# Spreading a row by one fp32 matmul, new shares in the first K'V, and later loads of a fourth batch

## The chip, the cores and the metric

The kernel runs on one core of one Trainium2 chip. A core has a matmul engine (TensorE, PE in the profile; its weight loads are PEld), three engines for elementwise work (VectorE or DVE, ScalarE or ACT, GpSimd or POOL), a queue engine (SyncE or SP) and 16 DMA engines that all queues share. The engines run side by side, each through its own list of instructions in order, and wait for each other through semaphores. The metric is the device time of one execution in microseconds (us); less is better. Before the change three runs took 333.25, 333.89 and 334.29 us.

## What is computed

Linear attention with cosine-weighted features, followed by a gated feed-forward layer:

```python
# attention: B, H, S, D = 8, 8, 576, 64
def phi(x, c, s):
    r = np.maximum(x, 0.0)
    return np.concatenate([r * c, r * s], axis=-1)
q_p = phi(q, cos_w, sin_w); k_p = phi(k, cos_w, sin_w)
kv  = np.einsum('bhsf,bhsd->bhfd', k_p, v)
z   = np.sum(k_p, axis=2)
num = np.einsum('bhsf,bhfd->bhsd', q_p, kv)
den = np.einsum('bhsf,bhf->bhs', q_p, z)[..., None] + 1e-06
x   = (num / den)              # as 4608 tokens x 512
# feed-forward: 512 -> 1536 -> 512
rms = np.sqrt(np.mean(x * x, axis=-1, keepdims=True) + 1e-06)
xn  = x / rms * rms_g
g, val = xn @ w_gate, xn @ w_val
out = (g * sigmoid(g) * val) @ w_out
```

## The kernel before

The 4608 tokens are handled as nine blocks of 512 tokens, each of four tiles of 128; block 8 collects the fifth half tiles of the batches. A block is 12 steps (`step`, L693): each makes one 128x512 piece of the gate product (`gps`) and of the value product (`vps`), applies silu on ScalarE (L714) and multiplies on VectorE (L724). From block 2 on each step also issues four matmuls of the output product of the block before (L520). Blocks 0 to 4 cut their steps into parts of 128 or 256 token columns (`PARTS`, L682), so that a block can start before all its tiles are there: block 1 (steps 12 to 23) works in steps 12 to 17 on tiles 0 and 1 and from step 18 on needs tiles 2 and 3 too.

Attention work of later batches is hung into these steps by a plan written by hand (`at`, L535): in step g, slot "pe" stands behind the step's matmuls, "dve0", "act1" and so on stand at places between. A tile goes through `num_mm` (product of turned q features and K'V, L379), `divide` (L417), `sumsq` (ScalarE squares, L428, then a power on GpSimd, L433), `norm` (L438, which multiplies by the gains `gb`) and a transpose of the normed tile, either on TensorE (`x_turn_pe`, L456, with an eviction) or as a DMA transpose on SP's queue (`x_turn`, L446). Turned q features come the same two ways (`q_turn_pe`, L355 and evictions L364 and L366; `q_turn`, a DMA transpose on SP, L344).

Loads of k, q and v (`load`, L112, each two DMAs) go to SP's queue for batch 0 and from batch 4 on, to GpSimd's queue for batches 1 and 2, and for batch 3 k and v go to GpSimd and q to SP. GpSimd's list holds nothing but constants, the weight loads, these loads and the powers of `sumsq`, in program order. k, q and v have two buffers each, used by even and odd batches. Between blocks 0 and 1 `lead` (L737) prepares batch 1, issues most of block 0's output matmuls, and issues the loads of batch 3's k and v.

The opening, ahead of step 0, prepares batch 0. VectorE builds the angle table, ScalarE takes its sine (L193), then both make k features (L271 and L269) and q features. Loads, features and K'V of batch 0 are cut in two halves of four heads (`HALVES`). TensorE runs 44 warming matmuls on constants meanwhile. The row of gains `rms_g` (1x512) has to stand on all 128 partitions: GpSimd splits it into three bf16 parts (L224, L226), three matmuls by a column of ones add them up on all partitions (L231), and ScalarE copies the sum into `gb` (L234). Then two q tiles are turned on TensorE; v is cast to bf16 (`v_cast`, tiles 0 to 2 on VectorE, L283, tiles 3 and 4 on ScalarE, L281); `kv_half` (L325) multiplies the five token tiles of four heads in the order 0, 1, 3, 2, 4 and evicts the half on VectorE (L337). ScalarE's copy of the second turned q tile (L366) stands between its casts of the two halves. Instructions recorded with `K` keep their program order on each engine.

Of the kernel before, what the change touches and what calls it, by code (L numbers as in the profile page):

```python
# [10 lines left out]
FP32 = mybir.dt.float32  # L11
BF16 = mybir.dt.bfloat16
AF = mybir.ActivationFunctionType
ALU = mybir.AluOpType
# [3 lines left out]
def kernel(  # L18
# [11 lines left out]
    nc = tc.nc  # L30
    B, H, S, D = q.shape
    DM = H * D
    DFF = moe_w_gate.shape[1]
    P = 128
# [12 lines left out]
    def K(i):  # L47
        tc.keep_in_program_order(i)
        return i

    consts = ctx.enter_context(tc.tile_pool(name="consts", bufs=1))
# [25 lines left out]
    def gv_tile(shape, dtype, name):  # L77
        u = gv_out.pop(0)
        t = ps_gv.tile(shape, dtype, name=name, tag=f"gv{u}")
        gv_in[id(t)] = (u, t)  # L80
        return t

    def gv_read(t):

        if id(t) in gv_in:
            gv_out.append(gv_in.pop(id(t))[0])
# [25 lines left out]
    def load(t, src, b, odd_five=False, cuts=(0, NC5), hs=slice(0, H), eng=None):  # L112
        if eng is None:
            eng = nc.gpsimd if 0 < b < 3 or b == 3 and src is not q else nc.sync
        for lo, hi in zip(cuts[:-1], cuts[1:]):
            for par, t0, jn in lanes(odd_five):
                z = min(hi, jn)
                if z <= lo:
                    continue
                K(eng.dma_start(  # L120
                    out=t[par:P:2, hs, lo * D : z * D],
                    in_=src[b, hs, :, :].rearrange("h (i j) d -> i h (j d)", j=NT)[
                        :, :, (t0 + lo) * D : (t0 + z) * D
                    ],
                ))

    def load_v(b, cuts=(0, NC5)):
        load(vraw[b], v, b, False, cuts)

    def load_k(b):  # L130
        load(kraw[b], k, b)
# [6 lines left out]
    clear_fifth(vbuf[0], nc.vector)  # L138
    gb = consts.tile([P, DM], FP32, name="gb")

    NX = 3
    xbuf = [consts.tile([P, DM + 1], FP32, name=f"x{u}") for u in range(NX)]
    g1, grest = xbuf[1][0:1, 0:DM], xbuf[2][0:1, 0:DM]
    K(nc.scalar.dma_start(out=g1, in_=moe_rms_g.rearrange("(o d) -> o d", o=1)))
    for hs in HALVES:
        load(kraw[0], k, 0, hs=hs)
# [1 line left out]
    for hs in HALVES:  # L148
# [14 lines left out]
        out=odd_i[:, :], in_=iota_i[:, :], scalar=1, op=ALU.bitwise_and  # L163
# [10 lines left out]
        out=iota_f[:, :], in0=iota_f[:, :], scalar1=J + 0.5, scalar2=None, op0=ALU.mult  # L174
    )
    for u, half in ((0, 0.5), (1, -0.5)):
        nc.vector.scalar_tensor_tensor(
            out=first[:, u : u + 1], in0=odd_f[:, :], scalar=half, in1=iota_f[:, :],
# [3 lines left out]
            out=th[:, 1, u * J : (u + 1) * J], in0=row_f[:, :],  # L182
# [3 lines left out]
        out=th[:, 1, 2 * J : NT], in0=first[:, 1:2],  # L186
# [3 lines left out]
        out=th[:, 0, :], in_=th[:, 1, :], scalar=math.pi / 2.0, op=ALU.add  # L190
# [14 lines left out]
    NK = 6  # L205
# [4 lines left out]
    kvm = [consts.tile([P, H, E], BF16, name=f"kvm{u}") for u in range(NK)]  # L210

    for u in range(NX):
        nc.gpsimd.memset(xbuf[u][:, DM : DM + 1], math.sqrt(1e-6 * DM))
    warm = consts.tile([P, 2 * P], BF16, name="warm")

    nc.vector.memset(warm[:, :], 1.0)
    for j in range(NC5):
        nc.gpsimd.memset(vx[j][:, :, D:E], 1.0)


    gpart = [kvm[NK - 1 - u][0:1, :, :].rearrange("p h e -> p (h e)")[:, 0:DM] for u in range(3)]
    for u in range(3):
        rest = g1 if u == 0 else grest
        K(nc.gpsimd.tensor_copy(out=gpart[u], in_=rest))  # L224
        if u < 2:
            K(nc.gpsimd.tensor_tensor(out=grest, in0=rest, in1=gpart[u], op=ALU.subtract))  # L226

    def spread_gains():
        ps = gv_tile([P, DM], FP32, "gains")
        for u in range(3):  # L230
            K(nc.tensor.matmul(  # L231
                ps[:, :], lhsT=warm[0:1, 0:P], rhs=gpart[u], start=(u == 0), stop=(u == 2)
            ))
        K(nc.scalar.copy(out=gb[:, :], in_=ps[:, :]))  # L234
        gv_read(ps)

# [38 lines left out]
    def k_feat(b, j, c, act=False, hs=slice(0, H)):  # L275
        feat(kp[j][:, hs, c, :], kraw[b][:, hs, j * D : (j + 1) * D], table(c, 0, j), act)

    def v_cast(b, j, act=False, hs=slice(0, H)):
        src, dst = vraw[b][:, hs, j * D : (j + 1) * D], vx[j][:, hs, 0:D]
        if act:  # L280
            K(nc.scalar.copy(out=dst, in_=src))  # L281
        else:
            K(nc.vector.tensor_copy(out=dst, in_=src))  # L283
# [18 lines left out]
    def kv_head(bank, j, h, start, stop):  # L302
        K(nc.tensor.matmul(  # L303
            bank[:, (h % Z) * E : (h % Z) * E + D + 1],
            lhsT=kp[j][:, h, :, :].rearrange("p c d -> p (c d)"),
            rhs=vx[j][:, h, 0 : D + 1],
            start=start, stop=stop,
        ))
# [16 lines left out]
    def kv_half(z, dve):  # L325

        bank = gv_tile([P, TB], FP32, "kv0")
        order = (0, 1, 3, 2, 4)
        for j in order:
            for h in range(z * Z, (z + 1) * Z):  # L330
                kv_head(
                    bank, j, h, j == order[0] and h % Z == 0, j == order[-1] and h % Z == Z - 1
                )
        src = bank[:, 0 : Z * E].rearrange("p (s w) -> p s w", w=E)[:, :, 0 : D + 1]
        dst = kvm[0][:, z * Z : (z + 1) * Z, 0 : D + 1]
        if dve:
            K(nc.vector.tensor_copy(out=dst, in_=src))  # L337
        else:
            K(nc.scalar.copy(out=dst, in_=src))
        gv_read(bank)  # L340
# [10 lines left out]
    def q_turn_pe(b, t):  # L351
        ps = gv_tile([P, H, P], BF16, "qtp")
        qp = qps.pop((b, t))
        for h in range(H):
            K(nc.tensor.transpose(  # L355
                ps[:, h, :], qp[:, h, :, :].rearrange("p c d -> p (c d)"), ident_b[:, :]
            ))
        qtp[b, t] = ps

    def q_evict(b, t, dve=False):  # L360
        tt = rqtp.tile([P, H, P], BF16, name="rqT", tag="rqT")
        ps = qtp.pop((b, t))
        if dve:
            K(nc.vector.tensor_copy(out=tt[:, :, :], in_=ps[:, :, :]))  # L364
        else:
            K(nc.scalar.copy(out=tt[:, :, :], in_=ps[:, :, :]))  # L366
        gv_read(ps)
        rqT[b, t] = tt
# [41 lines left out]
    def divide(key):  # L410
# [3 lines left out]
        r = recs.pop(key)[:, :].rearrange("p (z s) -> p z s", z=2)  # L414
        x = xbuf[nx[0] % NX]
        nx[0] += 1
# [118 lines left out]
    def at(g, w, f, *a):  # L535
        plan[g, w].append(lambda: f(*a))
# [100 lines left out]
        tile_at(22 + t, (2, t), 2, t)  # L637


    at(16, "pe", load_q, 3)  # L640
    for j in range(NC5):
        for c in range(2):
            at(22 + j, "act2" if c else "dve1", k_feat, 3, j, c, c == 1)
# [93 lines left out]
    def lead():  # L737

        for j in range(NC5):
            for c in range(2):  # L740
                k_feat(1, j, c, act=(j > 2))
        outs(0, 18)
        for t in range(2):
            for c in range(2):
                q_feat(1, t, c, act=(c == 1))
        q_turn_pe(1, 0)
        q_evict(1, 0, dve=True)
        outs(18, 21)
        q_turn_pe(1, 1)
        for j in range(NC5):  # L750
            v_cast(1, j, act=(j == 1))
        q_evict(1, 1)
        outs(21, 24)
        for j in range(NC5):
            kv_mm(1, j, j == 0, j == NC5 - 1)
        kv_evict(1)
        q_feat(1, 2, 0)
        q_feat(1, 2, 1, act=True)
        outs(24, 27)
        num_mm((1, 0))  # L760
        num_mm((1, 1))
        q_feat(1, 3, 1, act=True)
        divide((1, 0))
        sumsq((1, 0))
        outs(27, 31)
        q_turn_pe(1, 2)
        divide((1, 1))
        sumsq((1, 1))
        outs(31, 36)
        q_evict(1, 2, dve=True)  # L770
        q_feat(1, 3, 0)
        norm((1, 0))
        outs(36, 40)
        q_turn_pe(1, 3)
        load_k(3)
        load_v(3)
        x_turn_pe((1, 0))
        x_evict((1, 0), 1, 0, dve=True)
        q_evict(1, 3)
        outs(40, 45)  # L780
        norm((1, 1))
        x_turn_pe((1, 1))
        x_evict((1, 1), 1, 1, dve=True)
        for j in range(2):
            k_feat(2, j, 1, act=True)
        outs(45, 48)
        num_mm((1, 2))
# [4 lines left out]
    def warm_up(n):  # L792
        for _ in range(n):
            K(nc.tensor.matmul(
                wps[:, 0 : 2 * P], lhsT=warm[:, 0:P], rhs=warm[:, :], start=True, stop=True
            ))

    warm_up(44)
    for hs in HALVES:
        for j in range(NC5):  # L800
            for c in range(2):
# [7 lines left out]
    load_q(0, (J, NC5), eng=nc.gpsimd)  # L809
    for c in range(2):  # L810
        load_wo(c)
    spread_gains()
    q_turn_pe(0, 0)
    q_evict(0, 0, dve=True)
    q_turn_pe(0, 1)
    for z, hs in enumerate(HALVES):
        for j in range(NC5):
            v_cast(0, j, act=(j > 2), hs=hs)
        if z == 0:
            q_evict(0, 1)  # L820
        kv_half(z, True)
    num_mm((0, 0))
    num_mm((0, 1))
    for c in range(2):
# [27 lines left out]
    for c in range(2):  # L852
# [5 lines left out]
        for nn in range(NNT):  # L858
            K(nc.tensor.matmul(
                last[:, cs], lhsT=hT[B][:, nn, (J - 1) * P : J * P], rhs=wo[:, nn, cs],  # L860
                start=(nn == 0), stop=(nn == NNT - 1),
# [36 lines left out]
```

## Time and profile before

| what | value |
|---|---|
| three runs, median | 333.89 us (333.25 to 334.29) |
| the profiled execution | 332.95 us, of which the span is 331.1 us |
| first gate matmul of step 0 | 21.20 us after the span's start |
| TensorE between 9.84 us and 21.20 us | waits in six places |
| step 12 (block 1) starts | 59.48 us |
| step 18 starts | 71.07 us |
| DMA queue of SP (q1) | 72800 packets, 40.12 MB |
| DMA queue of GpSimd (q0) | 7168 packets, 14.29 MB |

How to read it: the span is what the profiler saw from the first instruction to the last; the run's time includes what lies around it. In the rows that follow, a line of the timeline gives start, duration, engine, source line, operation, tiles out and in, count, and in brackets the idle time ahead of it with what ended that. A line of the chain of waits gives start, length and the work that held up the end at that time. A row of DMA issues gives the tiles, the queue, the kind, how many, and the median time in us from issue to landing. A row of stretches gives the stretch, its length, busy time (with the count of instructions that touch it), granted TensorE clock, busy share of the DMA engines and GB/s.

### The profile page before, as it was taken

The numbers are of one execution on the slowest core, as the hardware profiler recorded it, in microseconds if no ns is written. First come the engines' busy times: TensorE is split into PE (matmuls) and PEld (weight loads), VectorE is DVE, ScalarE is ACT, GpSimd is POOL, SyncE is SP. The second block draws the span as 40 slices with busy tenths as digits, with TensorE's granted clock in tenths as the row PEclk, the third lists the DMA queues.
The fourth block names the chain that finished last, engine by engine and source line by source line (L and its number), as shares of the span: only waits on it lengthen the run. The fifth ranks groups of instructions, "written<-read, shape, count | busy, mean of one in ns | idle before, by whom it ended". The sixth has DMA issues, their size and how long they took to land.

```text
span 331.1 us, 7177 instructions
## 1 busy us (share of the span) xinstructions
PE 317.1 (96%) x2802; PEld 210.5 (64%) x2837; DVE 194.1 (59%) x403; ACT 168.8 (51%) x324; POOL 47.4 (14%) x90
## 2 busy tenths in 40 slices
PE   6679999999999999999999999999999999999995
PEld 4469966999887777778777644454444444444443
DVE  8786367777966585677867676746543422223200
ACT  3853477857864366575646564644432322322221
POOL 8664343200101000001110001000100000000000
PEclk9999999999999999999999999999999999999999
DMA  7999999994258999995799898254224020000012
GB/s 207 266 206 215 285 335 384 359 228 88 44 124 257 276 288 325 182 333 100 172 242 277 170 234 134 76 85 111 50 71 105 34 61 33 34 32 32 34 63 96
DMA packets 80164, 55.00 MB, mean 166 GB/s; under 512 B 51265, under 2 KB 73553, under 8 KB 80130
## 3 DMA queue, kind: packets, MB, share of 16 engines
q1 hardware_dynamic: 72800, 40.12, 50.1%
q0 software_dynamic: 7168, 14.29, 17.0%
q8 instruction: 22, 0.36, 0.5%
q10 hardware_dynamic: 162, 0.13, 0.1%
q14 instruction: 12, 0.10, 0.1%
HBM read 37.75 MB, written 9.44 MB: 142 GB/s over the span
## 4 chain that ended last, share of the span: by engine, by line
PE 86%; DVE 7%; issue 2%; DMA 2%; ACT 1%; POOL 0%; ACTq 0%; DVEq 0%
PE acc L520 26%; PE gps L488 14%; PE vps L488 14%; PE gps L475 12%; PE vps L475 12%; PE att L379 3%; PE att L303 3%; DMA xnT<-xn 2%; DVE kp L271 2%; DVE xn L438 1%; PE qtp L355 1%; PE xps L456 1%; DVE x L417 1%; DMA out_dram<-osb 1%; DVE vx L283 1%
## 5 line engine op out<-in xcount | busy, mean ns | idle before, releaser
L724 DVE TENSOR_TENSOR hT<-vps,sil 128x512 bf16<-128x512 f32 x108 | 74.5, 690 | 97.8 <-PE vps L475 58.0
L714 ACT ACTIVATE sil<-gps 128x512 bf16<-128x512 f32 x108 | 64.4, 596 | 98.6 <-PE gps L475 59.8
L520 PE MATMUL acc<-wo,hT 128*128 128x512 bf16 x396 | 101.8, 379 | 1.4 <-ACT osb L526 0.2
L520 PEld LDWEIGHTS <-hT 128*128 128x128 bf16 x420 | 40.5, 98 | 40.2 <-issue 0.3
L488 PE MATMUL gps<-xnT,wg 128*128 128x256 bf16 (+1 forms) x608 | 62.5, 250 | 1.2 <-DVE xnT L463 0.5
L488 PE MATMUL vps<-xnT,wv 128*128 128x256 bf16 (+1 forms) x608 | 62.5, 250 | 0.0
L488 PEld LDWEIGHTS <-wg 128*128 128x128 bf16 x608 | 48.0, 98 | 8.6 <-issue 1.2
L488 PEld LDWEIGHTS <-wv 128*128 128x128 bf16 x608 | 49.4, 98 | 4.1
L433 POOL TENSOR_TENSOR rs<-ss,mhalf 128x1 f32<-128x1 f32 x36 | 20.4, 567 | 197.0 <-ACT sq L428 197.0
L475 PE MATMUL gps<-xnT,wg 128*128 128x512 bf16 x139 | 36.7, 379 | 0.4
L475 PE MATMUL vps<-xnT,wv 128*128 128x512 bf16 x141 | 36.5, 379 | 0.1
L526 ACT COPY osb<-acc 128x512 f32<-128x512 f32 x35 | 20.5, 585 | 31.5 <-PE acc L520 28.7
L475 PEld LDWEIGHTS <-wv 128*128 128x128 bf16 x192 | 18.8, 98 | 22.7
L438 DVE SCALAR_TENSOR_TENSOR xn<-x,rs,gb 128x512 bf16<-128x512 f32 x36 | 26.9, 748 | 7.3 <-POOL rs L433 7.3
L475 PEld LDWEIGHTS <-wg 128*128 128x128 bf16 x192 | 18.0, 98 | 20.1
L428 ACT ACTIVATE sq<-x 128x513 f32<-128x513 f32 x36 | 22.6, 628 | 10.6 <-DVE x L417 8.6
L417 DVE TENSOR_TENSOR x<-att,rec 128x512 f32<-128x512 f32 x36 | 24.9, 691 | 1.3
L271 DVE TENSOR_SCALAR kp<-kbuf,trig 128x512 bf16<-128x512 f32 (+1 forms) x56 | 23.5, 457 | 0.6 <-PE att L303 0.3
L271 DVE TENSOR_SCALAR qp<-qbuf,trig 128x512 bf16<-128x512 f32 x50 | 22.8, 478 | 0.0
L269 ACT ACTIVATE kp<-kbuf,trig 128x512 bf16<-128x512 f32 (+1 forms) x34 | 21.4, 663 | 0.0
L269 ACT ACTIVATE qp<-qbuf,trig 128x512 bf16<-128x512 f32 x30 | 21.0, 712 | 0.4 <-DMA qbuf<-in_q_dram 0.4
L379 PEld LDWEIGHTS <-rqT 128*128 128x128 bf16 x320 | 14.3, 98 | 8.5 <-DVE rqT L364 1.4
(68 smaller groups left out, 195.1 us busy)
## 6 DMA issues: line engine op xcount, KB each, us to landing
out_dram<-osb SPq DMA_DIRECT2D x70, 128.0 KB, 2.1
qbuf<-in_q_dram SPq DMA_DIRECT2D x5, 640.0 KB, 6.2
qbuf<-in_q_dram SPq DMA_DIRECT2D x5, 512.0 KB, 5.0
kbuf<-in_k_dram SPq DMA_DIRECT2D x4, 640.0 KB, 6.4
vbuf<-in_v_dram SPq DMA_DIRECT2D x4, 640.0 KB, 6.9
kbuf<-in_k_dram SPq DMA_DIRECT2D x4, 512.0 KB, 5.3
vbuf<-in_v_dram SPq DMA_DIRECT2D x4, 512.0 KB, 6.1
kbuf<-in_k_dram POOLq DMA_DIRECT2D x3, 640.0 KB, 10.3
```

Source lines behind the costliest of these rows:

```text
L269: K(nc.scalar.activation(out=dst, in_=src, func=AF.Relu, scale=scale))
L271: K(nc.vector.tensor_scalar(out=dst, in0=src, scalar1=scale, scalar2=0.0, op0=ALU.mult, op1=ALU.max,))
L379: K(nc.tensor.matmul(nums[key][:, h // Z, (h % Z) * E : (h % Z) * E + D + 1], lhsT=rqT[a, t][:, h, :], rhs=kvm[a % NK][:, h, 0 : D + 1], s ...
L417: K(nc.vector.tensor_tensor(out=x[:, 0:DM].rearrange("p (z s d) -> p z s d", z=2, d=D), in0=a[:, :, :, 0:D], in1=r.unsqueeze(3).to_broadca ...
L428: K(nc.scalar.activation(out=sq[:, :], in_=xs[key][:, :], func=AF.Square, scale=1.0 / math.sqrt(DM), accum_out=ss[:, :],))
L438: K(nc.vector.scalar_tensor_tensor(out=xn[:, :], in0=xs.pop(key)[:, 0:DM], scalar=rss.pop(key)[:, :], in1=gb[:, :], op0=ALU.mult, op1=ALU. ...
L475: K(nc.tensor.matmul(ps[:, :], lhsT=w[:, dt, nn * P : (nn + 1) * P], rhs=xnT[blk][:, dt, :], start=(dt == 0), stop=(dt == NDT - 1),))
L488: K(nc.tensor.matmul(ps[:, i * cn : (i + 1) * cn], lhsT=w[:, dt, (n0 + i) * P : (n0 + i + 1) * P], rhs=xnT[blk][:, dt, c0 : c0 + cn], star ...
L520: K(nc.tensor.matmul(acc[blk][:, :], lhsT=hT[blk][:, nn, jt * P : (jt + 1) * P], rhs=wo[:, nn, :], start=(nn == 0), stop=(nn == NNT - 1),))
L526: K(nc.scalar.copy(out=osb[:, :], in_=acc[blk][:, :]))
L714: K(nc.scalar.activation(out=sil[:, :], in_=gp[:, :], func=AF.Silu))
L724: K(nc.vector.tensor_tensor(out=dst, in0=a, in1=c, op=ALU.mult))
```

## The change

The gains are spread by one fp32 matmul of a 1x128 row of ones by the 1x512 row itself; the five GpSimd operations that split the row are gone. It stands behind 14 warming matmuls, and 32 more follow, where 44 stood ahead of the three matmuls. So ScalarE's copy into `gb` now precedes its k features in the list. Of v's first half ScalarE casts three tiles and VectorE two; of the second half it stays two and three. The first half of K'V is evicted by ScalarE, the second by VectorE. The order of the token tiles is 0, 2, 1, 3, 4 in the first half and 0, 3, 1, 4, 2 in the second. Four warming matmuls stand ahead of K'V and four between its halves. ScalarE's copy of the second turned q tile comes behind both halves. The loads of batch 3: k and v move from `lead` to the ends of steps 16 and 17, q from step 16 to step 19. In GpSimd's list k's and v's four loads thus stand behind two more powers (tiles (1,2) and (1,3)); in SP's list q's two loads stand behind one more DMA transpose of q features.

```diff
-    g1, grest = xbuf[1][0:1, 0:DM], xbuf[2][0:1, 0:DM]
+    g1 = xbuf[1][0:1, 0:DM]
...
-    gpart = [kvm[NK - 1 - u][0:1, :, :].rearrange("p h e -> p (h e)")[:, 0:DM] for u in range(3)]
-    for u in range(3):
-        rest = g1 if u == 0 else grest
-        K(nc.gpsimd.tensor_copy(out=gpart[u], in_=rest))
-        if u < 2:
-            K(nc.gpsimd.tensor_tensor(out=grest, in0=rest, in1=gpart[u], op=ALU.subtract))
+    ones = consts.tile([1, P], FP32, name="ones")
+    nc.vector.memset(ones[:, :], 1.0)
 
     def spread_gains():
         ps = gv_tile([P, DM], FP32, "gains")
-        for u in range(3):
-            K(nc.tensor.matmul(
-                ps[:, :], lhsT=warm[0:1, 0:P], rhs=gpart[u], start=(u == 0), stop=(u == 2)
-            ))
+        K(nc.tensor.matmul(ps[:, :], lhsT=ones[:, :], rhs=g1, start=True, stop=True))
         K(nc.scalar.copy(out=gb[:, :], in_=ps[:, :]))
         gv_read(ps)
...
     def kv_half(z, dve):
-        order = (0, 1, 3, 2, 4)
+        order = (0, 3, 1, 4, 2) if z else (0, 2, 1, 3, 4)
...
-    at(16, "pe", load_q, 3)
+    at(16, "pe", load_k, 3)
+    at(17, "pe", load_v, 3)
+    at(19, "pe", load_q, 3)
...
         q_turn_pe(1, 3)
-        load_k(3)
-        load_v(3)
         x_turn_pe((1, 0))
...
-    warm_up(44)
+    warm_up(14)
+    spread_gains()
+    warm_up(32)
     for hs in HALVES:
         for j in range(NC5):
             for c in range(2):
...
     for c in range(2):
         load_wo(c)
-    spread_gains()
     q_turn_pe(0, 0)
     q_evict(0, 0, dve=True)
     q_turn_pe(0, 1)
+    warm_up(4)
     for z, hs in enumerate(HALVES):
         for j in range(NC5):
-            v_cast(0, j, act=(j > 2), hs=hs)
+            v_cast(0, j, act=(j > 2 - (z == 0)), hs=hs)
+        kv_half(z, z == 1)
         if z == 0:
-            q_evict(0, 1)
-        kv_half(z, True)
+            warm_up(4)
+    q_evict(0, 1)
     num_mm((0, 0))
```

## The prediction

> **What bounds the kernel now.** I read the page first (busy shares), then the chain of waits with its times, then the stretches where TensorE is not the bound: the opening (0 to 21 us) and one gap near 71 us.
>
> ```profile
> span 331.1 us, 7177 instructions
> PE 317.1 (96%) x2802; PEld 210.5 (64%) x2837; DVE 194.1 (59%) x403; ACT 168.8 (51%) x324; POOL 47.4 (14%) x90
> ```
>
> TensorE is busy 96% of the span, so only 14 us are open to any change that leaves its main work alone. The chain of waits says where they lie:
>
> ```profile
> 11.15 0.62 PE qtp L355 x8
> ...
> 12.40 0.81 DVE vx L283 x2
> ...
> 14.31 1.13 DVE vx L283 x3
> ...
> 15.48 0.43 PE kv L303 x8
> ...
> 15.93 0.44 DVE kvm L337
> ...
> 65.55 5.39 DMA xnT<-xn
> ```
>
> Until 21.20, where the first expert matmul starts, the chain runs on VectorE: key features, the copy of the turned q tile, six casts of v, two evictions of K'V, then divide and norm. After that it is TensorE, but for one DMA transpose, of tile (1,3), issued at 65.55 and landing at 70.94. The timeline shows what TensorE lost there, and what was issued around it:
>
> ```profile
> 60.04 1.11 SPq L510 DMA_DIRECT2D out_dram<-osb  x2
> 63.95 2.78 SPq L446 DMA_TRANSPOSE xnT<-xn  x2
> ...
> 64.18 0.55 POOL L433 TENSOR_TENSOR rs<-ss,mhalf 128x1 f32<-128x1 f32 x1 [1.76 <-ACT sq L428]
> ...
> 71.07 1.03 PE L488 MATMUL gps<-xnT,wg 128*128 128x256 bf16 x8 [0.45 <-DMA xnT<-xn]
> ```
>
> TensorE waited 0.45 us at step 18, so it would have started at 70.62. The ScalarE timeline of the opening:
>
> ```profile
> 10.23 1.32 ACT L269 ACTIVATE qp<-qbuf,trig 128x512 bf16<-128x512 f32 x2
> 11.46 0.56 ACT L234 COPY gb<-gains 128x512 f32<-128x512 f32 x1
> 11.92 0.71 ACT L281 CAST vx<-vbuf 128x256 bf16<-128x256 f32 x2
> 12.54 1.00 ACT L366 COPY rqT<-qtp 128x1024 bf16<-128x1024 bf16 x1
> ```
>
> Start to start, a q feature costs 0.62 us here, the copy of the gains 0.46, a cast 0.31, the q copy 0.90.
>
> **The change, part by part.** *Splitting of the row.* Five GpSimd operations between 2.08 and 7.83 go. GpSimd's next deed with a follower is the probe at 11.07, which waits for VectorE's q feature, so this is worth nothing; if the probe waited for GpSimd, it would be worth up to 4 us of GpSimd's time. The memset of ones sits in VectorE's angle chain, which ends in the sine at 6.77: between 0.10 us (a 128x1 memset) and 0.27 (the 128x256 one); I take 0.1.
>
> *The fp32 matmul.* No fp32 matmul stands in this trace. The warming matmuls price the clock of that moment by their starts (the granted clock reads 1.00 throughout):
>
> ```profile
> 3.50:4.50 1.00, 1.00 (x7) 1.00 1.03 358
> ...
> 8.50:9.50 1.00, 1.00 (x12) 1.00 1.06 375
> ```
>
> All 44 take 7.03 us, early ones some 0.21 us apart, late ones 0.11, so 14 end near 5.75. Below, fp32 costs one 512-column pass at the early rate, 0.42. Above, both operands in three bf16 parts make nine products, 3.8. The nearest row is the three passes that it replaces (0.82 us late, twice that early); I take 1.3 for a place where the rate changes: done at 7.1. The copy of the gains now stands ahead of all key features on ScalarE, behind the sine (6.77 plus 0.1 and 0.22), so those start at 7.2 + 0.46 = 7.66 and not 7.02: 0.64 later. ScalarE had the time idle, 4.22 us ahead of the sine, but the order puts the copy behind it.
>
> [...]
>
> *Casts and evictions.* ScalarE's first q feature now ends at 10.89 + 0.64 = 11.53, so the turn of q tile 0 starts at 11.58 instead of 11.15, and VectorE, which copies it first, begins its casts at 12.83 instead of 12.40. It has two, then three, and no eviction between: at 0.36 each the first half's end at 13.60, the second's at 14.68 (15.44 before). ScalarE's second q feature ends at 12.15, its three casts near 13.1. TensorE then has 12 of 20 matmuls left (0.69 us for 16, so some 0.5 with their latency): K'V of the first half at 14.15, its eviction on ScalarE until 14.6 (0.43, by VectorE's row), then ScalarE's two casts until 15.26. The last eight matmuls take 0.43: eviction of the second half at 15.73 and not 15.93. That is -0.2 us on the chain. Behind ScalarE's wait for K'V stand its two casts, which TensorE then waits for, and the q copy (ends 16.2, just when its product is due). Bounds: with ScalarE out of the way VectorE's casts alone set it, 12.40 + 5 x 0.36 = 14.2 against 15.44, -1.2; with the 3.8 us matmul ScalarE is 2.5 us later still, +2.
>
> *Warming matmuls.* Two more ahead, four and four between: eight at 0.11 fall into TensorE's waits (1.33 us for the vx casts at 12.75 and 14.74). Cost 0; without that cover, 0.45 us each four.
>
> *Loads of batch 3.* Four K and V loads on GpSimd's queue (56.45 to 59.22) are moved behind the two powers of tiles (1,2) and (1,3). GpSimd waits for no step, only for its own order: they issue from the end of that power, 64.73, until 67.5, not in steps 16 and 17 proper. Each takes 0.69 us to issue. q's two loads move behind one rqT transpose on SP that starts at 76.39: landing near 78 + 6.6, while its first reader is at 86.60; K and V have first readers at 81.11. Both fit, so nothing is late there. What matters is step 18. The second transpose issues at 65.55, 0.8 us behind the first K load, as both hang on the same power. Landing times, issue to landing, of the same transpose:
>
> ```profile
> xnT<-xn SPq DMA_TRANSPOSE x3, 7.0
> ...
> xnT<-xn SPq DMA_TRANSPOSE x5, 2.4
> ```
>
> The first is from 110 to 130 us, among loads; the second from 200 to 240, quiet. The two stores at 60.04 took 7.4 us beside these same K and V loads, against 2.1 as the page's median: 5.3 more. Quiet, it lands at 67.95 and the 0.45 us go: the bound below. With 5.3 more on 2.4 it lands at 73.25. I take 7.3, the longest of the three transposes: 72.85, a wait of 2.23 at step 18, 1.78 more than now. The gap widens, since 2.3 MB at the 355 GB/s seen take 6.6 us from about 66.5. The rqT transpose behind it (landing 4.9 now) is needed at 75.99, later still by then.
>
> Sum: -0.2 + 1.78 = +1.6 us. The profiled execution took 332.95 (span 331.1 and 1.85 around it); it would take 334.5. The median of the runs shown, 333.89, is 0.94 above it, so I forecast 335.5.
>
> **The rivals.** *Quick transposes* (not slower): the second transpose is through before K's packets come, or takes turns with them without loss. [...] Against: the stores at 60.04. It gives -0.2 - 0.45 = -0.65, 333.2. [...]
>
> *Quick transposes and a free ScalarE* (faster): if the fp32 pass is over before the sine and ScalarE's operations end sooner, the opening gains up to 1.2: -1.2 - 0.45 = -1.65, 332.2.
>
> *A long fp32 matmul* (slower, in another place): from 2.6 us on, the copy of the gains holds ScalarE's key features past 8.9, and TensorE's turn of q past 12.8. At 3.8 us: +2 - 0.45 = +1.55, 335.4.
>
> *The loads stay where they were*, because GpSimd runs ahead: excluded, since two powers stand before them.
>
> **How the numbers follow.** Transpose caught behind K and V (forecast) 0.50, 335.5, its own range 334.3 to 337.2; quick transposes 0.18, 333.2; with free ScalarE 0.20, 332.2; long matmul 0.12, 335.4. The range reaches from 332.4 to 337.2: below lies a part of the third case, above the two slow cases together. A change within 0.3% (1.0 us) can't be told from none. Faster by more: the third case and a little of the second, 0.22; slower by more: the first and fourth but for their low ends, 0.60; between, 0.18.
>
> **What would show it.** Right: the two xnT transposes of 63.95 and 65.55 land over 6 us after issue, and the first gps matmul of step 18 waits 2 us or more for DMA. Wrong: that wait is gone. The opening is read at the first gps matmul (21.20), the copy of gb (behind the sine, at 7.2), the second K'V eviction (15.73). A second wait at the product of tile (2,0) would add to it. If the total rises with these as before, a load of batch 3 came late for its first reader.

## The result and the profile after

The changed kernel takes 344.15 us (median of 6 runs, 343.62 to 345.91) where the kernel before took 334.03 (333.25 to 334.94) beside it: a ratio of 1.0316, interval 1.0284 to 1.0349. Forecast were 335.5 us and at most 337.2. Comparisons leave out disturbed executions; one of these is the profiled execution of the run after_kv_sp below, which is why no view of that run is read.

The profiled execution took 345.82 us. Its page, busy time by engine and the granted clock in 40 slices of 8.6 us:

```profile
span 344.1 us, 7192 instructions
...
PE 322.7 (94%) x2811; PEld 213.5 (62%) x2846; DVE 190.7 (55%) x402; ACT 169.5 (49%) x326; POOL 43.4 (13%) x85
...
PE   6979999935999999999999999999999999999995
...
PEclk9999999995999999999999999999999999999999
```

The span is 13.0 us longer, TensorE's busy time only 5.6. In the ninth and tenth slice (69 to 86 us) TensorE stands idle and then runs at a lower clock. The chain of waits (start, length, what held up the end) has that stretch as one DMA transpose, and the opening above it:

```profile
2.81 3.17 PE wps L786 x14
5.98 2.00 PE gains L225 x2
7.98 5.28 PE wps L786 x32
13.26 0.46 PE qtp L347 x8
...
22.44 1.05 PE gps L480 x16
...
66.79 14.70 DMA xnT<-xn
81.49 0.14 issue
81.63 1.87 PE gps L480 x8
83.49 1.71 PE vps L480 x8
85.20 1.87 PE att L295 x40
87.06 0.87 PE gps L480 x8
```

The transpose of tile (1,3) was issued at 66.79 and landed 14.70 us later, where it took 5.39 before. Behind it eight gate matmuls take 1.87 us, eight value matmuls 1.71, and 40 of K'V 1.87; in the chain of the kernel before the same three are 1.03, 0.87 and 1.27. The timeline names the partners (times, engine, line, tiles; in brackets the idle time ahead):

```profile
65.20 2.78 SPq L438 DMA_TRANSPOSE xnT<-xn  x2
...
65.93 1.50 POOL L120 DMA_DIRECT2D kbuf<-in_k_dram  x2
...
67.43 1.37 POOL L120 DMA_DIRECT2D vbuf<-in_v_dram  x2
...
81.63 1.87 PE L480 MATMUL gps<-xnT,wg 128*128 128x256 bf16 x8 [9.77 <-DMA xnT<-xn]
```

The first transpose landed in 2.5 us, ahead of the loads' packets. The second met them. The view of DMA issues (queue, kind, count, KB, us from issue to landing) shows that both sides lost:

```profile
kbuf<-in_k_dram POOLq DMA_DIRECT2D x1, 640.0 KB, 9.2
vbuf<-in_v_dram POOLq DMA_DIRECT2D x1, 640.0 KB, 13.5
...
rqT<-qp SPq DMA_TRANSPOSE x1, 14.1
```

V's second load, issued near 68.1, landed near 81.6, just as the transpose did (81.49). The DMA engines had work meanwhile. The stretches (length, busy time of each engine, clock, DMA share, GB/s), first after, then before:

```profile
60.00:72.00 12.00, 11.86 (x211) 11.41 (x209) 10.15 (x22) 8.04 (x16) 3.92 (x6) 1.00 0.56 126
72.00:81.00 9.00, 0.00 (x0) 0.00 (x0) 1.66 (x4) 0.82 (x2) 0.00 (x0) 0.74 1.01 175
81.00:90.00 9.00, 8.37 (x91) 7.11 (x92) 2.10 (x6) 3.45 (x7) 0.00 (x0) 0.70 0.10 14
```

```profile
60.00:72.00 12.00, 11.55 (x203) 11.31 (x201) 10.47 (x22) 7.95 (x16) 1.11 (x2) 1.00 1.15 277
```

From 72 to 81 us they show a full share of busy time, yet move 175 GB/s; before, at a like share, 277. So packets took longer, rather than waiting for work. The loads' packets can be priced: the views of 60 to 85 us (queue, packets, MB, share of 16 engines' time) of the changed kernel and of turns_on_pe below, where the loads meet no transpose, are

```profile
q0 software_dynamic: 576, 2.36, 42.7%
```

```profile
q0 software_dynamic: 576, 2.36, 28.0%
```

The share times 25 us times 16 engines, over 576 packets, is 0.30 us for one packet beside the transposes and 0.19 without them.

The balance of the profiled 13.0 us: the wait at step 18, 9.77 less 0.45, is 9.3; the low clock behind it 0.84 + 0.84 + 0.60 = 2.3; the first gate matmul 22.44 - 21.20 = 1.2. That is 12.8. It is the balance of two executions: the medians are 10.1 apart, the one profiled after is 1.7 above its median, the one before (332.95) below its own. The 1.2 of the opening is not shown to come from the change: with the opening as it was, the executions profiled below have that first gate matmul between 21.58 (turns_on_pe) and 22.31 (kv_gated).

### The profile page after: what moved, and what is told of

Read it like the earlier page. It is cut to its first block, busy times and chain, and to the rows that moved or that the text cites. A ratio compares the mean times of both kernels' runs of the same rounds, so it can differ in the third digit from the quotient of the medians.

```text
span 344.1 us, 7192 instructions
## 1 busy us (share of the span) xinstructions
PE 322.7 (94%) x2811; PEld 213.5 (62%) x2846; DVE 190.7 (55%) x402; ACT 169.5 (49%) x326; POOL 43.4 (13%) x85
## 4 chain that ended last, share of the span: by engine, by line
PE 85%; DMA 7%; DVE 4%; issue 2%; ACT 1%; POOL 0%; ACTq 0%; DVEq 0%
PE acc L512 24%; PE gps L480 13%; PE vps L480 13%; PE gps L467 12%; PE vps L467 12%; DMA xnT<-xn 4%; PE att L371 3%; PE wps L786 2%; PE att L295 2%; DMA rqT<-qp 2%; DVE xn L430 1%; PE qtp L347 1%; PE xps L448 1%; DVE x L409 1%; PE gains L225 1%
## 5 line engine op out<-in xcount | busy, mean ns | idle before, releaser
L480 PE MATMUL gps<-xnT,wg 128*128 128x256 bf16 (+1 forms) x608 | 63.3, 252 | 10.6 <-DMA xnT<-xn 9.8
L480 PE MATMUL vps<-xnT,wv 128*128 128x256 bf16 (+1 forms) x608 | 63.4, 252 | 0.0
```

Source lines behind the costliest of these rows:

```text
L480: K(nc.tensor.matmul(ps[:, i * cn : (i + 1) * cn], lhsT=w[:, dt, (n0 + i) * P : (n0 + i + 1) * P], rhs=xnT[blk][:, dt, c0 : c0 + cn], star ...
```

## The experiments

Twelve kernels ran; all compute the whole output. Ratios, with 95% intervals, are to the kernel before, run beside them.

**Which part loses the time.** loads_only is the kernel before with the loads moved and nothing else:

```diff
-    at(16, "pe", load_q, 3)
+    at(16, "pe", load_k, 3)
+    at(17, "pe", load_v, 3)
+    at(19, "pe", load_q, 3)
...
-        load_k(3)
-        load_v(3)
```

> The kernel before with the loads of batch 3 moved to steps 16, 17 and 19 and nothing else changed. Theory A (the second transpose of step 18 shares the DMA engines with K's and V's loads and is starved, and TensorE's clock falls after the long wait): some 9 us of wait and 2 us of slow matmuls as in the changed kernel, so 334.0 + 11.5 = 345.5. Rival (the collision needs the opening's shift, the move alone does little): within 2 us of before.

Measured: 343.79 us, ratio 1.030 (1.0268 to 1.0332): the whole loss. Its chain, and V's second load, issued near 67.6:

```profile
66.24 13.17 DMA xnT<-xn
...
vbuf<-in_v_dram POOLq DMA_DIRECT2D x1, 640.0 KB, 11.9
```

opening_only is the changed kernel with these lines put back.

> The changed kernel with the loads of batch 3 put back where they were. Theory A: only the opening's 1.24 us remain, first gate matmul at 22.4, step 18 waits 0.45 as before: 335.2. Rival: the opening carries most of the loss: over 340.

Measured: 334.06 us, ratio 0.9994 (0.9971 to 1.0017). All of the opening's edits together are worth nothing that can be told. Its profiled execution had the first gate matmul at 23.58, after_filled below, with the same opening, at 20.93: one execution's opening says little.

**Is it the meeting of loads and transposes, and does it go by bytes?** v_only moves only V:

```diff
+    at(17, "pe", load_v, 3)
     at(16, "pe", load_q, 3)
...
-        load_v(3)
```

> The kernel before with only V's load of batch 3 moved to step 17; K's stays in the lead, q's in step 16. Theory A with a loss that goes with the bytes in the way: half the bytes, so the second transpose lands some 8 us after issue (14.7 with K and V, 2.4 with none), a wait near 3 us and no or little loss of clock: 336.5. Rival (any meeting holds the transpose for a fixed time): as with both loads, 343.

Measured: 337.73 us, ratio 1.0108 (1.0076 to 1.0141). Half the bytes, and the same transpose takes 7.69 us:

```profile
66.00 7.69 DMA xnT<-xn
73.83 1.87 PE gps L488 x8
...
vbuf<-in_v_dram POOLq DMA_DIRECT2D x1, 640.0 KB, 7.4
```

V's second load, issued near 65.9, landed 7.4 us later, so at 73.3, and the transpose at 73.69. In these three kernels the transpose lands within 0.4 us of the end of the other queue's loads (81.49 and 81.6, 79.41 and 79.5, 73.69 and 73.3): its time is no price of its own. After a wait of 2.8 us TensorE's clock was low again (granted 0.72 from 72 to 78 us).

kv_gated holds K and V of batch 3 back until the transposes have landed: a GpSimd read of the turned q tile (2,0) stands ahead of them.

```diff
+    at(16, "pe", lambda: pool_after(rqT[2, 0][0:1, 0, 0:1]))
+    at(16, "pe", load_k, 3)
+    at(16, "pe", load_v, 3)
     at(16, "pe", load_q, 3)
...
-        load_k(3)
-        load_v(3)
```

> The kernel before with K's and V's loads of batch 3 held on GpSimd's queue until the DMA transpose of q tile (2,0), the last of the three in a row, has landed (a one-element copy from it stands ahead of them); q's load stays in step 16. Theory A: the transposes run alone and land 2.4 us after issue, the loads land by 80 us, ahead of their readers at 81.1; the 0.45 us wait at step 18 goes: 333.5. Rival (later loads are late for batch 3's features): slower than before by 1 us or more, with a wait of TensorE near step 22 to 28.

Measured: 339.0 us, ratio 1.0149 (1.0107 to 1.019), where 333.5 was expected. Step 18 was freed, but the timeline shows the loads meeting the next transpose:

```profile
72.32 1.65 POOL L120 DMA_DIRECT2D kbuf<-in_k_dram  x2 [0.33 <-issue]
...
73.95 1.36 POOL L120 DMA_DIRECT2D vbuf<-in_v_dram  x2
...
76.89 8.09 SPq L344 DMA_TRANSPOSE rqT<-qp  x3
...
85.34 0.62 PE L379 MATMUL att<-kvm,rqT 128*128 128x65 bf16 x8 [3.12 <-DMA rqT<-qp]
```

That transpose landed at 85.3, V's second load near 84.5. The expectation had asked only when the loads start, not what else is issued until they end.

after_filled is the changed kernel with 80 more warming matmuls behind step 17, to hold the clock through the wait.

```diff
+    at(17, "pe", fill, 80)
```

> The changed kernel with 80 warming matmuls behind step 17, so that TensorE works through most of the wait at step 18. Theory A says that some 2.2 us of the loss are matmuls at half rate after the wait: the transpose still lands at 81.5, but the next steps run at the full rate: 344.15 - 2.2 = 342. Rival (the slow matmuls have another cause, such as contention): no change, 344.

Measured: 342.76 us, ratio 1.0276 (1.0227 to 1.0325), with the granted clock at 1.00 throughout. That is 1.4 us less than the changed kernel's 344.15, but the two intervals overlap, and in the profiled execution the transpose itself landed sooner: 13.4 us after its issue, near 78.7, some 1.6 us ahead of V's second load. What holding the clock saves of the 2.3 us read above is thus not settled. The wait itself stays, now filled with work that nobody needs.

**Is it the two queues?** kv_on_sp is loads_only with K and V on SP's queue, where they stand behind the transposes issued so far:

```diff
-            eng = nc.gpsimd if 0 < b < 3 or b == 3 and src is not q else nc.sync
+            eng = nc.gpsimd if 0 < b < 3 else nc.sync
```

> The kernel before with the loads in steps 16, 17 and 19, K and V on SP's queue, behind the three transposes and ahead of the next. Theory A (two queues at once on the same engines starve the transposes): in one queue they go one after the other, step 18 has no wait, 333.5 to 334. Rival (any K and V bytes at that time starve the transposes): a wait of several us at step 18 or 19, over 338.

Measured: 333.37 us, ratio 0.9995 (0.9978 to 1.0012). The same bytes, issued from 69.29 to 72.75 and so some 4 us later than in loads_only, and everything is quick:

```profile
kbuf<-in_k_dram SPq DMA_DIRECT2D x1, 640.0 KB, 6.0
vbuf<-in_v_dram SPq DMA_DIRECT2D x1, 640.0 KB, 8.6
...
xnT<-xn SPq DMA_TRANSPOSE x2, 2.5
```

Even the 0.45 us wait of the kernel before is gone. The edit changes the queue and, with it, the order: three transposes had been issued before the first load. The next one, issued at 76.83 behind the loads on the same queue, landed 4.6 us later, near 81.4, again just behind V's second load (near 80.6), but in time for its reader. So one queue does not free a transpose from the loads ahead of it; what is gone is the slowing of the loads (8.6 us for V's second, as turns_on_pe's 8.5 below). No run here has the loads on GpSimd's queue in this same order and at this time, so queue and order are not told apart beyond that. turns_on_pe leaves the loads on GpSimd's queue and turns tiles (1,2) and (1,3) and q tile (2,0) on TensorE instead (the edit for the q tile is left out here):

```diff
...
-        at(g, "sp", x_turn_late, (1, t), 1, t)
+        at(g + 1, "pe", x_turn_pe, (1, t))
+        at(g + 2, "dve0", x_evict, (1, t), 1, t, True)
```

> The kernel before with the loads moved to steps 16, 17 and 19, and the three transposes that meet them (normed tiles (1,2) and (1,3), q tile (2,0)) made on TensorE with evictions on VectorE. Theory A (the loss is the meeting of DMA transposes and GpSimd's loads, not the loads' lateness): no wait for DMA at step 18, K and V land within 10 us; the added turns cost TensorE some 0.9 us: 334.5. Rival (the loads come too late for batch 3, or slow everything by themselves): over 338.

Measured: 334.55 us, ratio 1.0022 (1.0008 to 1.0036). Without those transposes the loads land in 4.3 to 8.5 us from GpSimd's queue too; what the turns cost TensorE is not read apart from that ratio. after_kv_sp applies the edit of kv_on_sp to the changed kernel.

> The changed kernel with one thing put right: K and V of batch 3 are issued in steps 16 and 17 on SyncE's queue, behind the transposes, and not on GpSimd's. If the whole loss is the meeting of two queues: 333.4 to 334.4, no DMA wait at step 18 over 0.5 us, transposes of tiles (1,2) and (1,3) landing in about 2.5 us, granted clock 1.00 after 60 us. If anything else of the change costs time (opening, clock), it stays above 335.

Measured: 333.53 us (332.06 to 334.62), ratio 0.9981 (0.996 to 1.0001). One word about a queue takes back the 10 us.

**What the opening could give.** gains_late is the kernel before with the split gone, the fp32 matmul between the halves of K'V and the copy of the gains behind ScalarE's features of q tile (0,2).

```diff
-    spread_gains()
     q_turn_pe(0, 0)
...
+        if z == 0:
+            gains_mm()
...
+    gains_copy()
```

> The kernel before with the splitting on GpSimd gone and one fp32 matmul, but placed between the halves of K'V, its copy behind ScalarE's q features of tile 2, where ScalarE has 2 us to spare. In the changed kernel VectorE's angle chain ended at 4.1 us instead of 6.8, which is read as GpSimd's split operations having slowed it. If so, and the copy is off ScalarE's path, the opening is shorter by 0.5 to 1 us: 333.2. Rival (the opening is set by the loads of q and v landing): no change, 333.9. The fp32 matmul itself should take 0.9 us there at the full clock, by the two records of 2.07 us together in the changed kernel at the low one.

Measured: 333.69 us, ratio 1.0005 (0.9987 to 1.0023): no gain, where 333.2 was expected. The matmul took 2.07 us there and not the 0.9 expected, at a granted clock of 0.50 (14 to 16 us). gains_behind is after_kv_sp with the matmul behind all 46 warming matmuls and the copy behind ScalarE's features of the first two q tiles; copy_behind differs from it only in the matmul's place.

```diff
-    warm_up(14)
-    spread_gains()
-    warm_up(32)
+    warm_up(46)
+    gains_mm()
...
+    gains_copy()
     pool_after(qps[0, 0][0:1, 0, 0, 0:1])
```

> As the run before, but the fp32 matmul stands behind all 46 warming matmuls, and the copy of the gains behind ScalarE's two q features. Theory: the fp32 matmul lets TensorE's rate fall, so that the 32 warming matmuls behind it end late (13.26) and hold the turn of q tile 0. Then here the warming matmuls end before 11, the turn starts at ScalarE's q feature (11.2 to 11.6), the first expert matmul starts 0.5 to 1.5 us earlier than in the run before at the same granted clock, and the time is some 0.5 to 1 us less. Rival: the rate in the opening goes by itself and not by the fp32 matmul; then the warming matmuls are as slow, and the times agree within 0.3%.

> As gains_behind, but the fp32 matmul is back between the 14 and the 32 warming matmuls; only the copy of the gains stays behind ScalarE's q features. Theory: the matmul's place decides, since behind it TensorE stays at its low rate in some executions (fp32 2.07 us, the 32 behind it 5.3 us and more); then 333.3 to 334, as after_kv_sp. Rival: what gains_behind won is the copy, which no longer holds ScalarE's key features; then 331.7 to 332.4. Either way K and V of batch 3 are on SyncE's queue: no DMA wait at step 18 over 0.5 us and the transposes of tiles (1,2) and (1,3) land in under 4 us.

Measured: gains_behind 332.02 us, ratio 0.9958 (0.9934 to 0.9983), faster than both kernels; copy_behind 333.7 us (331.74 to 335.15), ratio 0.9989 (0.9966 to 1.0012). The timelines of TensorE, gains_behind first, copy_behind second:

```profile
2.81 7.24 PE L792 MATMUL wps<-warm 128*128 128x256 bf16 x46 [2.81 <-DVE warm L217]
9.99 1.12 PE L228 MATMUL gains<-x,ones 1*128 1x512 f32 x2
11.04 1.07 PE L353 MATMUL qtp<-ident_b,qp 128*128 128x128 bf16 x16
...
20.22 1.46 PE L486 MATMUL gps<-xnT,wg 128*128 128x128 bf16 x16 [0.52 <-DVE xnT L461]
```

```profile
2.81 3.17 PE L792 MATMUL wps<-warm 128*128 128x256 bf16 x14 [2.81 <-DVE warm L217]
5.91 2.07 PE L228 MATMUL gains<-x,ones 1*128 1x512 f32 x2
7.91 5.44 PE L792 MATMUL wps<-warm 128*128 128x256 bf16 x32
13.19 1.06 PE L353 MATMUL qtp<-ident_b,qp 128*128 128x128 bf16 x16
...
22.43 1.05 PE L486 MATMUL gps<-xnT,wg 128*128 128x128 bf16 x16 [0.52 <-DVE xnT L461]
```

The same instructions, but with the matmul behind the others it takes 1.12 us and the q turn starts at 11.04; in front, 2.07 and 13.19. In these two traces the place decides, and copy_behind doesn't show that the copy alone wins. But the intervals of the two ratios overlap, and after_filled had 1.12 us with the matmul in front (last section), so neither the rule nor the size of the difference (0.3%) is settled. In the profiled execution of gains_behind the granted clock fell just then (0.68 from 20 to 22 us, 0.50 to 24; its first gate matmuls take 1.46 us), which gives part of it back.

sp_and_late joins kv_on_sp and gains_late, with four warming matmuls in each of two gaps.

```diff
     q_turn_pe(0, 1)
+    warm_up(4)
...
             gains_mm()
+            warm_up(4)
```

> The kernel before with K and V of batch 3 on SyncE's queue in steps 16 and 17 and q in 19, the split of the row gone, the fp32 matmul and four warming matmuls between the halves of the first K'V and four ahead of it. If the earlier angles and the 0.45 us of step 18 add up: 332.5 to 333.2, faster than both kernels. If the opening goes by the granted clock, as runs of either part alone suggest: 333.3 to 334, no change that can be told.

Measured: 333.02 us, ratio 0.9977 (0.9954 to 0.9999): perhaps 0.2%, and not to be told from gains_behind, whose interval overlaps.

## Why the prediction was wrong

**The place was right.** The loads issued from 65.93 and the second transpose at 66.79; the forecast had 64.73 and 65.55, and both moved by the opening's 1.2 us. TensorE waited at step 18, for that transpose, caught behind K and V, while the first was quick. loads_only shows that this is the whole loss; turns_on_pe, without the transposes, and kv_on_sp, with the loads behind them, that it is the meeting.

**The step that failed** is the landing: "I take 7.3, the longest of the three transposes", and from it "a wait of 2.23 at step 18". It measured 14.70 and 9.77. The row was of the wrong kind. Those three transposes, between 110 and 130 us, stand among loads of batches from 4 on, which go to SP's own queue (GpSimd's moves nothing in that stretch); there, as in kv_on_sp, transpose and load stand in one queue. The stores at 60.04, 7.4 us, did meet GpSimd's loads, but are no transposes. The row that bore on it was the 5.39 us of the chain of waits itself: that transpose still met the tail of V, whose second load was issued near 58.5 in the kernel before:

```profile
vbuf<-in_v_dram POOLq DMA_DIRECT2D x1, 640.0 KB, 10.4
```

So V landed near 69, and the transpose at 70.94, two us after it, where kv_on_sp's landed in 2.5 us. I read 5.39 as a duration; by these rows it was an end time that the other queue had a part in. With all of K and V ahead, the end to reckon with was that of V.

**A second error enlarged it.** "2.3 MB at the 355 GB/s seen take 6.6 us from about 66.5" would have put V's end at 73.1. It came at 81.6, since the transposes slow the loads as well: V's second load took 13.5 us, in turns_on_pe without transposes 8.5, and a packet 0.30 us where it took 0.19 there.

**A term was missing:** TensorE's clock after the wait (granted 0.70 from 81 to 90 us), 2.3 us in the profiled execution. The low clock came with a wait of 2.8 us too (v_only, 0.72 from 72 to 78 us); whether 2.23 would have brought it, no run shows.

**The rivals.** *Quick transposes* is refuted: the second transpose was not through before K's packets came, and if the queues took turns, it was not without loss, 14.70 us to its landing and 13.5 to that of V's second load. In the stretch from 62 to 84 us GpSimd's queue moved 2.36 MB in 576 packets, SP's 0.79 MB in 2304. That does not tell how the two shared the engines, nor why hardly a packet began between 71.9 and 73 us (29 and 20 GB/s in two slices of 0.55 us, busy tenths 1 and 0, as this view books a packet's time where it begins), with three loads and two transposes outstanding. Why the packets took longer stays open.

**The opening** nets nothing, as -0.2 us would have looked, but not by its terms. The fp32 matmul took 2.07 us, not 1.3, and the 32 warming matmuls behind it 0.165 us each, not 0.11; they end at 13.26 and hold the turn of q tile 0, forecast for 11.58. *A long fp32 matmul* is refuted at 3.8 us, but its mechanism, a late turn, occurred by way of the matmuls behind it. "This is worth nothing", of GpSimd's split, was wrong as far as the traces show: VectorE's angle chain ran beside it, and was slower there. Before, with the GpSimd line that ran at the time of the second, and after:

```profile
2.75 1.33 DVE L167 CAST row_f<-row_i 128x4 f32<-128x4 int32 x1
...
5.21 1.52 DVE L189 TENSOR_SCALAR th<-th 128x9 f32<-128x9 f32 x1
...
5.56 1.14 POOL L226 TENSOR_TENSOR x<-x,kvm 1x512 f32<-1x512 f32 x1
```

```profile
2.89 0.32 DVE L168 CAST row_f<-row_i 128x4 f32<-128x4 int32 x1
...
3.93 0.17 DVE L190 TENSOR_SCALAR th<-th 128x9 f32<-128x9 f32 x1
...
8.02 0.59 ACT L226 COPY gb<-gains 128x512 f32<-128x512 f32 x1 [3.66 <-PE gains L225]
8.50 3.30 ACT L261 ACTIVATE kp<-kbuf,trig 128x256 bf16<-128x256 f32 x8
```

The sine could start at 4.14 instead of 6.77. The changed kernel had no use of it: ScalarE stood 3.66 us before the copy of the gains, and its features began at 8.50, later than the 7.02 of before. *A free ScalarE* was thus to be had by another order: gains_behind, with 332.02, is near that rival's 332.2, though with the loads on SP's queue and not by quick transposes beside them.

## What to carry to other kernels

In these runs a DMA transpose that met loads of another queue landed within two us of the end of those loads (from 1.6 us ahead of it in after_filled to 2 us behind it in the kernel before), and made them later (V's second load 13.5 us in the changed kernel, 8.5 in turns_on_pe); so when a load is moved, list what every other queue issues until its end, and try the loads behind the transposes on one queue where they fit. A landing time is taken from rows with the same pairing of queues, and asked whether it is a duration or another transfer's end. To a wait of several microseconds on TensorE (2.8 was enough here, with a granted clock of 0.72 behind it), add the clock behind it.

## What the runs showed unasked

TensorE's rate and the granted clock are not one thing: in the changed kernel 7 warming matmuls touch each microsecond from 8.5 to 11.5 and 12 the one from 11.5, all at a granted clock of 1.00. With the fp32 matmul behind 14 of them, three of four profiled executions stayed at the low rate behind it (5.3 to 6.5 us for 32). The fourth, after_filled, did not:

```profile
2.81 3.13 PE L795 MATMUL wps<-warm 128*128 128x256 bf16 x14 [2.81 <-DVE warm L217]
5.88 1.12 PE L225 MATMUL gains<-x,ones 1*128 1x512 f32 x2
6.93 3.67 PE L795 MATMUL wps<-warm 128*128 128x256 bf16 x32
```

There the rate had risen by the fp32 matmul, which took 1.12 us as in gains_behind. The rise came at another moment in each of these executions: with no fp32 matmul among the warming ones, between 6.5 and 7.5 us in the kernel before and in gains_behind (9 matmuls touch that microsecond, 12 the next), some 4 us after the first at 2.81; with it, near 6 in after_filled, at 11.5 in the changed kernel, and not by 13.5 in opening_only. What sets the moment, and whether the fp32 matmul puts it off, no run here separates.

Four small VectorE operations took 1.15 to 1.52 us beside GpSimd's subtractions of the split, and 0.17 to 0.32 in the changed kernel without them.
